# Pooled attention and an MLP on one core: k by halves of its heads on 96 partitions, v by DMAs of 128 partitions, the last row tile in parts

## Chip, core and metric

One core of a Trainium2 chip. The metric is the device time of one execution in microseconds (us); lower is better. All data lies in the chip's HBM at the start and the result has to be there at the end.

## What is computed

```python
B, H, S, D = 8, 8, 576, 64;  pool = 8                    # float32 inputs
k_p = k.reshape(B, H, S // pool, pool, D).mean(axis=3)   # 72 pooled rows per head
v_p = v.reshape(B, H, S // pool, pool, D).mean(axis=3)
scores = matmul(q, k_p.T) / sqrt(D)
attn = softmax(scores)
x = matmul(attn, v_p)            # 4608 tokens x 512, heads side by side
h = x @ w_in                     # 512 -> 2048
out = gelu_tanh(h) @ w_out       # 2048 -> 512, float32
```

## The kernel before, in words

The batch has 8 parts (b) of 576 tokens, 4608 tokens in all. The MLP works on 9 groups (g) of 512 tokens. For a group, p1 (`p1_mm`, L333) multiplies by w_in: 16 column tiles (fo) times 4 tiles of the contraction (ko), each a matmul of 128x512, with the Gelu on ACT after each fo. p2 (`p2_mm`, L344) multiplies by w_out: 4 row tiles (r) times 16 fo, and `store` (L348) copies a row tile out of PSUM on DVE and sends it to HBM by four DMAs of 32 rows. All of it is written out by hand: `tc.manual_schedule()` keeps each engine's instructions in the order in which the program issues them, so a wait holds whatever is behind it on that engine.

The attention of batch g + 1 is laid between the matmuls of group g: pooling of k and v on DVE and the transposes of k on TensorE during p1 (the dictionary `plan`, L463 and L466), scores, exponentials and products during p2 (the list `pos`, L501). Batch 0 has no group before it. It stands ahead of the loop (L364 to L434), and there TensorE is kept busy with matmuls that nobody reads (`spin`, L359).

Names that matter:

- `load_k`, `load_v`, `load_q` (L67 to L88) bring one batch's k, v, q. In k, 4 pooled rows' inputs (4 x 2 KB) lie on one partition of `kts` (128 partitions, columns 0 to 3); the remaining 64 rows and v's last pooled rows take a fifth column. v is loaded in two DMAs of 64 partitions each, the lower heads on partitions 0 to 63, the upper on 64 to 127. For batch 0 k and v are issued from SP and ACT and q from GpSimd (POOL), which converts to bfloat16 on the way; for all other batches everything is issued from POOL.
- POOL's queue after that (L107 to L113): w_in in two halves, k, q, v of batch 1, then w_out in four quarters. The first eight DMAs go out at once; a ninth waits until the first has landed, and so on, since eight semaphores are used in turn.
- `k_steps` (L141): three additions on DVE that fold 8 rows to 1, into `kps`. `trans_k_mm` (L170) transposes `kps` on TensorE, `trans_k_copy` (L176) copies the result into `kTs`, twice (e = 0 and 1), in six pieces each. `v_steps` (L155) folds v into `vps` (batch 0: `vz`); `v_moves` (L149), from SP, moves v's last pooled rows.
- Batch 0: `qk`/`expo` give the scores and exponentials of a head pair, `den0` the sums by a matmul with `ones`, `inverse0` 1/sum on ACT (logarithm and exponential), `av0` the product with v, `mult0` the multiply on DVE into `xT`. After the last `mult0` (L426) DVE clears buffers for the later batches (L427 to L434), and after those comes batch 1's `k_steps`.
- In group 0 the first two row tiles of p2 go by quarters of w_out (L516), so that each quarter is asked for as late as possible.

Of the kernel before, what the change touches and what calls it, by code (L numbers as in the profile page):

```python
# [8 lines left out]
F32 = mybir.dt.float32  # L9
# [9 lines left out]
def kernel(  # L19
# [9 lines left out]
    nc = tc.nc  # L29
# [13 lines left out]
    KR = 4  # L43
# [20 lines left out]

    kts = [consts.tile([128, KR + 1, 512], F32, name=f"kt{i}") for i in range(2)]

    def load_k(b, engs):  # L67
        rows = k[b].rearrange("h (j l) d -> (h j) (l d)", l=8)
        main = rows[0:128 * KR].rearrange("(p r) c -> p r c", r=KR)
        n = KR // len(engs)  # L70
        for i, eng in enumerate(engs):
            eng.dma_start(out=kts[b % 2][:, i * n:(i + 1) * n], in_=main[:, i * n:(i + 1) * n])
        engs[0].dma_start(out=kts[b % 2][64:128, KR], in_=rows[128 * KR:])
        rows = v[b].rearrange("h (j l) d -> j h (l d)", l=8)
        for i in range(2):
            engs[-1].dma_start(out=kts[b % 2][32 * i:32 * i + 32, KR], in_=rows[64:, 4 * i:4 * i + 4])

    def load_v(b, engs):
        rows = v[b].rearrange("h (j l) d -> j h (l d)", l=8)
        for i in range(2):  # L80
            engs[i % len(engs)].dma_start(out=vts[b % 2][64 * i:64 * i + 64], in_=rows[0:64, 4 * i:4 * i + 4])  # L81
# [16 lines left out]
    load_k(0, [nc.sync, nc.scalar])  # L98
    load_v(0, [nc.sync, nc.scalar])
    load_q(0, 0, 1)  # L100
    load_q(0, 1, 2)
# [7 lines left out]
    load_k(1, [nc.gpsimd])  # L109
    load_q(1)  # L110
    load_v(1, [nc.gpsimd])
    for i in range(4):
        nc.gpsimd.dma_start(out=w_out_b[:, 4 * i:4 * i + 4, :].rearrange("p j d -> p (j d)"), in_=w_out_v[:, i])  # L113
# [6 lines left out]
    kps = [consts.tile([128, KR + 2, D], BF16, name=f"kp{i}") for i in range(2)]  # L120
# [6 lines left out]
    nc.vector.memset(idle, 0.0)  # L127
    nc.vector.memset(kTs[0][0], 0.0)
# [9 lines left out]
    def add(o, a, b):  # L138
        nc.vector.tensor_tensor(out=o, in0=a, in1=b, op=ALU.add)  # L139

    def k_steps(b, c=slice(0, KR + 1)):  # L141


        t = kts[b % 2]
        return [lambda: add(t[:, c, 0:256], t[:, c, 0:256], t[:, c, 256:512]),
                lambda: add(t[:, c, 0:128], t[:, c, 0:128], t[:, c, 128:256]),
                lambda: add(kps[b % 2][:, c], t[:, c, 0:64], t[:, c, 64:128])]

    def v_moves(b):  # L149

        for i in range(2):
            nc.sync.dma_start(out=vps[b % 2][64 - 64 * i:72 - 64 * i, 4 * i:4 * i + 4, 0],
                              in_=kps[b % 2][32 * i:32 * i + 32, KR])
# [13 lines left out]
    def half_bank(bank):  # L167
        return PS[:, bank, :].bitcast(BF16)

    def trans_k_mm(b, bank, r0=0, r1=KR + 1, n=128):  # L170
        tp = half_bank(bank)[:, 0:(KR + 1) * 128].rearrange("p (r c) -> p r c", c=128)
        kf = kps[b % 2].rearrange("p r d -> p (r d)")
        for r in range(r0, r1):
            nc.tensor.transpose(out=tp[:n, r, :], in_=kf[:, r * D:r * D + n], identity=identb)  # L174

    def trans_k_copy(b, e, bank, lower=True, upper=True):  # L176


        tp = half_bank(bank)[0:D, 0:(KR + 1) * 128].rearrange("p (r c) -> p r c", c=128)
        o = kTs[b % 2][e][e * 64:(e + 1) * 64]  # L180
        copy = nc.vector.tensor_copy

        def heads(h0, h1, c0, j0, j1):
            copy(out=o[:, h0:h1, c0:c0 + (j1 - j0) * KR].rearrange("p h (j r) -> p h j r", r=KR),  # L184
                 in_=tp[:, 0:KR, h0 * KH:h1 * KH].rearrange("p r (h j) -> p h j r", j=KH)[:, :, j0:j1])

        if lower:
            heads(0, 4, 0, 0, KH)
        if upper:
            heads(4, H - 1, 64, 0, 16)  # L190
            heads(4, H - 1, 0, 16, KH)
            copy(out=o[:, H - 1, 64:72].rearrange("p (j r) -> p j r", r=KR),
                 in_=tp[:, 0:KR, (H - 1) * KH:128].rearrange("p r j -> p j r"))
            copy(out=o[:, H - 1, 72:128], in_=tp[:, KR, 64:120])
            copy(out=o[:, H - 1, 0:8], in_=tp[:, KR, 120:128])

    def trans_k(b, bank):
        trans_k_mm(b, bank)
        for e in range(2):
            trans_k_copy(b, e, bank)  # L200
# [143 lines left out]
    def p2_mm(g, r, fo):  # L344
        nc.tensor.matmul(out=PS[:, o_bank(g, r), :], lhsT=gTs[g][:, fo, r * 128:(r + 1) * 128], rhs=w_out_b[:, fo, :],  # L345
                         start=(fo == 0), stop=(fo == FO - 1))

    def store(g, r):  # L348
        osb = opool.tile([128, DM], F32, name="osb")
        nc.vector.tensor_copy(out=osb, in_=PS[:, o_bank(g, r), :])  # L350

        for n in range(4):
            b, c = divmod(g * GROUP + r * 128 + n * 32, S)
            rows = out[b * S:(b + 1) * S].rearrange("(p t e) d -> e t p d", t=TP, e=2)
            eng = nc.scalar if (g, r) == (NG - 1, 3) and n % 2 else nc.sync
            eng.dma_start(out=rows[c // CH, c % CH // 32], in_=osb[n * 32:(n + 1) * 32, :])
# [8 lines left out]
    spin(22, 1)  # L365
    for f in k_steps(0, slice(0, KR)):
        f()
# [5 lines left out]
    trans_k_mm(0, 4, 0, KR, D)  # L373
    trans_k_copy(0, 0, 4, upper=False)
    trans_q(0, *QG[0], 5, nc.scalar)
    trans_q(0, *QG[1], 6, nc.vector)
    trans_k_copy(0, 1, 4, upper=False)
# [3 lines left out]
    for f in k_steps(0, slice(KR, KR + 1)):  # L381
        f()
    scores(1, 0, 2)
    trans_k_mm(0, 4, KR, KR + 1, D)
    trans_k_copy(0, 0, 4, lower=False)

    for h in range(H):
        i = h // 4
        nc.tensor.matmul(out=PS[64 - 64 * i:72 - 64 * i, 7, h * D:(h + 1) * D],
                         lhsT=identb[0:64, 32 * i + h % 4:32 * i + 32:4], rhs=kps[0][0:64, KR],  # L390
                         start=True, stop=True)
# [9 lines left out]
    trans_k_copy(0, 1, 4, lower=False)  # L401
# [9 lines left out]
    spin(4, 4)  # L411
    av0(0, 0, 4)
    mult0(0, 0, 4)
    den0(0, 2, 2)
    inverse0(0, 2, 2)
    av0(1, 0, 0)
    mult0(1, 0, 0)
    spin(3, 6)
    den0(1, 2, 6)
    inverse0(1, 2, 6)  # L420
    spin(3, 4)
    av0(0, 2, 4)
    mult0(0, 2, 4)
    spin(3, 0)
    av0(1, 2, 0)
    mult0(1, 2, 0)  # L426
    for t in kps:  # L427
        nc.vector.memset(t[:, KR + 1], 0.0)
# [11 lines left out]
    for g in range(NG):  # L440
# [3 lines left out]
        def load_next():  # L444

            load_q(g + 2)
            trans_q_dma(g + 2)
            nc.gpsimd.tensor_copy(out=gate, in_=qTs[g + 2][0:1, 1, TP - 1, 0:2])  # L448
            load_k(g + 2, [nc.gpsimd])
            load_v(g + 2, [nc.gpsimd])  # L450
# [62 lines left out]
        seq = [(r, fo) for r in range(4) for fo in range(FO)]  # L513
# [3 lines left out]
        for m, (r, fo) in enumerate(seq):  # L517
            for f, a in todo.pop(m, []):
                f(*a)
            p2_mm(g, r, fo)  # L520
            if fo == FO - 1:
                store(g, r)
        for m in sorted(todo):
            for f, a in todo[m]:
                f(*a)

# [29 lines left out]
```

The softmax here doesn't subtract the row's maximum and nothing guards it: scores larger than these inputs give would overflow.

## Time and profile before

| | us |
|---|---|
| median of 3 runs | 308.79 (308.76 to 308.96) |
| the profiled execution | 308.29 |
| its span in the profile | 306.5 |
| TensorE busy | 298.2 (97% of the span) |
| ACT busy | 219.0 (71%) |
| DVE busy | 150.4 (49%) |
| POOL busy | 36.3 (12%) |
| first matmul of p1 starts | 22.08 |
| last matmul ends | 302.1 |

The 1.8 us between span and execution lie around what the profile shows. A busy TensorE is not a TensorE at its peak: the idle spins count as busy too. In the timeline a line has start, duration, engine, line of the kernel, operation, what is written and read, and in brackets the idle time ahead of it and what ended it. In the chain of waits a piece has start, duration and what the time went to. PE is TensorE, PEld its weight loads, DVE VectorE, ACT ScalarE, POOL GpSimd, SP SyncE; a q behind a name is the engine's own queue of DMAs and semaphores.

### The profile page before, as it was taken

The numbers are of one execution on the slowest core, as the hardware profiler recorded it, in microseconds if no ns is written. First come the engines' busy times: TensorE is split into PE (matmuls) and PEld (weight loads), VectorE is DVE, ScalarE is ACT, GpSimd is POOL, SyncE is SP. The second block draws the span as 40 slices with busy tenths as digits, with TensorE's granted clock in tenths as the row PEclk, the third lists the DMA queues.
The fourth block names the chain that finished last, engine by engine and source line by source line (L and its number), as shares of the span: only waits on it lengthen the run. The fifth ranks groups of instructions, "written<-read, shape, count | busy, mean of one in ns | idle before, by whom it ended". The sixth has DMA issues, their size and how long they took to land.

```text
span 306.5 us, 4325 instructions
## 1 busy us (share of the span) xinstructions
PE 298.2 (97%) x1518; PEld 157.4 (51%) x1548; DVE 150.4 (49%) x334; ACT 219.0 (71%) x402; POOL 36.3 (12%) x69
## 2 busy tenths in 40 slices
PE   8999999999999999999999999999999999999994
PEld 3555555555555555555555555555555555445441
DVE  5868557573677057806681559245933630110021
ACT  1686679868987798779977998789868987206400
POOL 7103002305004000220014000400000000000000
PEclk9999999999999999999999999999999999999999
DMA  7999996987957952596159725662101210121022
GB/s 225 266 257 253 214 186 137 299 176 177 269 146 167 247 122 51 114 282 156 34 112 266 168 56 106 200 151 71 35 1 36 63 41 2 34 70 34 2 70 68
DMA packets 30359, 41.12 MB, mean 134 GB/s; under 512 B 18113, under 2 KB 18113, under 8 KB 29441
## 3 DMA queue, kind: packets, MB, share of 16 engines
q0 software_dynamic: 7856, 25.43, 34.9%
q1 hardware_dynamic: 21888, 14.09, 19.2%
q10 hardware_dynamic: 592, 1.31, 1.2%
q8 instruction: 12, 0.20, 0.3%
q14 instruction: 11, 0.08, 0.1%
HBM read 36.70 MB, written 9.44 MB: 151 GB/s over the span
## 4 chain that ended last, share of the span: by engine, by line
PE 83%; DMA 12%; POOL 1%; issue 1%; ACT 0%; DVE 0%; POOLq 0%
PE PS L345 38%; PE PS L336 36%; DMA kt<-in_k_dram 7%; DMA w_out_b<-in_moe_w_out_dram 5%; PE PS L239 4%; PE PS L261 4%; PE PS L174 1%; POOL w_in_b L105 0%; POOL qb L86 0%; POOL w_out_b L113 0%; DVE osb L350 0%; ACT e L247 0%; ACT ld L269 0%; ACT ld L268 0%; POOL identb masks.py:199 0%
## 5 line engine op out<-in xcount | busy, mean ns | idle before, releaser
L345 PE MATMUL PS<-w_out_b,gT 128*128 128x512 bf16 x560 | 134.2, 379 | 0.9
L336 PE MATMUL PS<-xT,w_in_b 128*128 128x512 bf16 x563 | 126.2, 379 | 0.6
L342 ACT ACTIVATE gT<-PS 128x512 bf16<-128x512 f32 x144 | 81.1, 604 | 47.5 <-PE PS L336 47.4
L336 PEld LDWEIGHTS <-w_in_b 128*128 128x128 bf16 x576 | 64.7, 113 | 57.2
L345 PEld LDWEIGHTS <-gT 128*128 128x128 bf16 x576 | 56.1, 97 | 56.7 <-issue 1.1
L350 DVE COPY osb<-PS 128x512 f32<-128x512 f32 x36 | 24.9, 691 | 98.3 <-PE PS L345 95.3
L279 DVE TENSOR_TENSOR xT<-PS,rc 64x288 bf16<-64x288 f32 x112 | 51.0, 455 | 31.6 <-ACT rc L271 29.3
L247 ACT ACTIVATE e<-PS 72x576 bf16<-72x576 f32 (+1 forms) x64 | 41.0, 646 | 9.1 <-PE PS L239 8.2
L239 PE MATMUL PS<-qT,kT 128*72 128x288 bf16 (+1 forms) x128 | 25.9, 286 | 0.9 <-ACT qT L214 0.6
L271 ACT ACTIVATE rc<-ld 128x288 f32<-128x288 f32 x56 | 24.8, 443 | 1.8
L314 ACT ACT_TABLE_LOAD x17 | 21.8, 1283 | 4.3 <-issue 4.1
L268 ACT ACTIVATE ld<-PS 64x288 f32<-64x288 f32 x56 | 22.8, 407 | 1.3
L269 ACT ACTIVATE ld<-PS 64x288 f32<-64x288 f32 x56 | 22.5, 402 | 1.3
L261 PE MATMUL PS<-e,vp 72*128 72x288 bf16 (+1 forms) x112 | 23.1, 286 | 0.0
L139 DVE TENSOR_TENSOR kt<-kt 128x1280 f32<-128x1280 f32 (+5 forms) x18 | 18.8, 1044 | 5.5 <-DMA kt<-in_v_dram 2.6
L239 PEld LDWEIGHTS <-kT 128*72 128x72 bf16 (+1 forms) x128 | 13.2, 105 | 15.2 <-DVE qT L216 1.2
L448 POOL COPY gate<-qT 1x2 bf16<-1x2 bf16 x6 | 1.0, 174 | 140.0 <-DMA qT<-qb 140.0
L139 DVE TENSOR_TENSOR vt<-vt 128x1024 f32<-128x1024 f32 (+1 forms) x16 | 15.3, 956 | 1.8 <-DMA vt<-in_v_dram 1.5
L184 DVE COPY kT<-PS 64x288 bf16<-64x288 bf16 (+2 forms) x48 | 13.0, 319 | 6.2 <-PE PS L174 6.1
L362 PE MATMUL PS<-idle 128*128 128x512 bf16 x39 | 11.9, 447 | 1.2 <-DVE idle L127 1.2
L261 PEld LDWEIGHTS <-vp 72*128 72x128 bf16 (+1 forms) x112 | 11.0, 98 | 3.8
L81 POOL DMA_DIRECT2D vt<-in_v_dram x14 | 9.0, 655 | 7.5 <-DMA w_in_b<-in_moe_w_in_dram 5.5
(47 smaller groups left out, 90.0 us busy)
## 6 DMA issues: line engine op xcount, KB each, us to landing
out_dram<-osb SPq DMA_DIRECT2D x142, 64.0 KB
kt<-in_k_dram POOLq DMA_DIRECT2D x7, 1024.0 KB, 6.2
vt<-in_v_dram POOLq DMA_DIRECT2D x14, 512.0 KB, 8.6
qb<-in_q_dram POOLq DMA_DIRECT2D x7, 576.0 KB, 11.6
w_in_b<-in_moe_w_in_dram POOLq DMA_DIRECT2D x2, 1024.0 KB, 16.7
w_out_b<-in_moe_w_out_dram POOLq DMA_DIRECT2D x4, 512.0 KB, 13.9
kt<-in_k_dram POOLq DMA_DIRECT2D x7, 128.0 KB, 5.9
kt<-in_v_dram POOLq DMA_DIRECT2D x14, 64.0 KB, 5.7
```

The lines of the kernel that those rows point to most:

```text
L139: nc.vector.tensor_tensor(out=o, in0=a, in1=b, op=ALU.add)
L239: nc.tensor.matmul(out=PS[:n, bank + e, :CH].rearrange("j (t p) -> j t p", p=32), lhsT=kTs[b % 2][c][:, h, :n], rhs=qTs[b][:, h // 4, :, h ...
L247: nc.scalar.activation(out=e[:n], in_=PS[:n, bank:bank + 2, :CH], func=ACT.Exp, scale=1.0 / 64.0)
L261: nc.tensor.matmul(out=PS[:, bank + x, :CH], lhsT=window(vps[b % 2][:n], 2 * pr + x), rhs=e[:n, x, :], start=True, stop=True)
L268: nc.scalar.activation(out=ld[0:64], in_=PS[64:128, bank, :CH], func=ACT.Ln)
L269: nc.scalar.activation(out=ld[64:128], in_=PS[0:64, bank + 1, :CH], func=ACT.Ln)
L271: nc.scalar.activation(out=rc, in_=ld, func=ACT.Exp, scale=-1.0)
L279: nc.vector.tensor_tensor(out=xT[rows, pr, col:col + CH], in0=PS[rows, bank + x, :CH], in1=rc[rows], op=ALU.mult)
L336: nc.tensor.matmul(out=PS[:, h_bank(g, fo), c0:c1], lhsT=w_in_b[fo // 8][:, ko, q * 512 + j:(q + 1) * 512:4], rhs=xT[:, ko, r0 + c0:r0 + c ...
L342: nc.scalar.activation(out=gTs[g][:, fo, :], in_=PS[:, h_bank(g, fo), :], func=ACT.Gelu_apprx_tanh)
L345: nc.tensor.matmul(out=PS[:, o_bank(g, r), :], lhsT=gTs[g][:, fo, r * 128:(r + 1) * 128], rhs=w_out_b[:, fo, :], start=(fo == 0), stop=(fo ...
L350: nc.vector.tensor_copy(out=osb, in_=PS[:, o_bank(g, r), :])
```

## The change

- **k.** Three pooled rows' inputs lie on a partition now, so each half of the heads takes 96 partitions. The lower heads go to partitions 0 to 95, columns 0 to 2; the upper heads to partitions 32 to 127, columns 3 to 5. v's last pooled rows are on partitions 0 to 31, columns 3 and 4. For batch 0 the lower half is issued from SP and ACT, beside q's first half from POOL; the upper half follows q's first half on POOL. The parts of `kts` that no load writes are cleared by DVE.
- **Pooling and transposes of k.** The additions take 3 columns per half in batch 0, and 6 columns otherwise (5 before). There are 6 transposes per batch instead of 5; the copies are 5 pieces instead of 6.
- **Batch 0's order.** q's first half is transposed before k, both copies of it on ACT; 13 + 3 spins instead of 22 at the start; k's upper half is summed where the fifth column was; one `den0`/`inverse0` pair moves ahead of the first `av0`, and the spins between the later products become fewer.
- **v.** Four DMAs, one for a head of each half, of 128 partitions.
- **w_out.** Its first quarter is issued ahead of batch 1's v.
- **The last row tile** of the last group: columns 0 to 383 for all fo, then 384 to 511, each with its own copy and stores. The first part's four stores go to SP, the second part's to SP and ACT by turns.

```diff
-    KR = 4
+    KR = 3
     KH = Sp // KR
...
+    kts = [consts.tile([128, 2 * KR, 512], F32, name=f"kt{i}") for i in range(2)]
+    K0 = (0, 32)
+
+    def load_k(b, i, engs):
+        rows = k[b].rearrange("(i h) (j r l) d -> i (h j) (r l d)", i=2, r=KR, l=8)[i]
+        n = 4 * KH // len(engs)
+        for x, eng in enumerate(engs):
+            eng.dma_start(out=kts[b % 2][K0[i] + x * n:K0[i] + (x + 1) * n, KR * i:KR * i + KR],
+                          in_=rows[x * n:(x + 1) * n].rearrange("p (r c) -> p r c", r=KR))
+
+    def load_v_last(b, eng):
         rows = v[b].rearrange("h (j l) d -> j h (l d)", l=8)
         for i in range(2):
-            engs[-1].dma_start(out=kts[b % 2][32 * i:32 * i + 32, KR], in_=rows[64:, 4 * i:4 * i + 4])
+            eng.dma_start(out=kts[b % 2][0:32, KR + i], in_=rows[64:, 4 * i:4 * i + 4])
 
     def load_v(b, engs):
-        rows = v[b].rearrange("h (j l) d -> j h (l d)", l=8)
-        for i in range(2):
-            engs[i % len(engs)].dma_start(out=vts[b % 2][64 * i:64 * i + 64], in_=rows[0:64, 4 * i:4 * i + 4])
+        rows = v[b].rearrange("(i h) (j l) d -> h i j (l d)", i=2, l=8)
+        for h in range(4):
+            engs[h % len(engs)].dma_start(out=vts[b % 2][:, h], in_=rows[h, :, 0:64])
...
-    load_k(0, [nc.sync, nc.scalar])
+    load_k(0, 0, [nc.sync, nc.scalar])
+    load_q(0, 0, 1)
+    load_k(0, 1, [nc.gpsimd])
+    load_v_last(0, nc.scalar)
+    load_q(0, 1, 2)
     load_v(0, [nc.sync, nc.scalar])
-    load_q(0, 0, 1)
-    load_q(0, 1, 2)
...
-    load_k(1, [nc.gpsimd])
+    load_k_all(1)
     load_q(1)
-    load_v(1, [nc.gpsimd])
     for i in range(4):
+        if i == 1:
+            load_v(1, [nc.gpsimd])
         nc.gpsimd.dma_start(out=w_out_b[:, 4 * i:4 * i + 4, :].rearrange("p j d -> p (j d)"), in_=w_out_v[:, i])
...
+    nc.vector.memset(kts[0][0:32, 2 * KR - 1], 0.0)
...
     act_set(EXP_SET)
-    spin(22, 1)
-    for f in k_steps(0, slice(0, KR)):
+    spin(13, 1)
+    for f in k_steps(0, 0, 1):
         f()
...
-    trans_k_mm(0, 4, 0, KR, D)
-    trans_k_copy(0, 0, 4, upper=False)
     trans_q(0, *QG[0], 5, nc.scalar)
-    trans_q(0, *QG[1], 6, nc.vector)
-    trans_k_copy(0, 1, 4, upper=False)
+    trans_q(0, *QG[1], 6, nc.scalar)
+    spin(3, 4)
+    trans_k_mm(0, 0, 4)
+    trans_k_copy(0, 0, 0, 4)
+    trans_k_copy(0, 1, 0, 4)
     scores(0, 0, 2)
     scores(0, 1, 0)
     spin(2, 7)
-    for f in k_steps(0, slice(KR, KR + 1)):
+    for f in k_steps(0, 1, 2):
         f()
     scores(1, 0, 2)
-    trans_k_mm(0, 4, KR, KR + 1, D)
-    trans_k_copy(0, 0, 4, lower=False)
+    trans_k_mm(0, 1, 4)
+    trans_k_copy(0, 0, 1, 4)
...
     inverse0(1, 0, 6)
-    spin(4, 4)
+    spin(2, 4)
+    den0(0, 2, 2)
+    inverse0(0, 2, 2)
+    spin(2, 4)
     av0(0, 0, 4)
     mult0(0, 0, 4)
-    den0(0, 2, 2)
-    inverse0(0, 2, 2)
+    den0(1, 2, 6)
+    inverse0(1, 2, 6)
     av0(1, 0, 0)
     mult0(1, 0, 0)
-    spin(3, 6)
-    den0(1, 2, 6)
-    inverse0(1, 2, 6)
-    spin(3, 4)
     av0(0, 2, 4)
     mult0(0, 2, 4)
-    spin(3, 0)
+    spin(2, 0)
     av0(1, 2, 0)
     mult0(1, 2, 0)
     for t in kps:
-        nc.vector.memset(t[:, KR + 1], 0.0)
+        nc.vector.memset(t[:, 2 * KR], 0.0)
+    for t in kts:
+        nc.vector.memset(t[96:128, 0:KR], 0.0)
+    nc.vector.memset(kts[1][0:32, 2 * KR - 1], 0.0)
...
-            eng = nc.scalar if (g, r) == (NG - 1, 3) and n % 2 else nc.sync
-            eng.dma_start(out=rows[c // CH, c % CH // 32], in_=osb[n * 32:(n + 1) * 32, :])
+            eng = nc.scalar if c1 == DM and c0 and n % 2 else nc.sync
+            eng.dma_start(out=rows[col // CH, col % CH // 32, :, c0:c1], in_=osb[n * 32:(n + 1) * 32, c0:c1])
...
+        seq = [(r, fo) for r in range(4 if g + 1 < NG else 3) for fo in range(FO)]
...
+    for c0, c1, bank in ((0, 384, o_bank(g, 3)), (384, DM, 4)):
+        for fo in range(FO):
+            p2_mm(g, 3, fo, bank, c0, c1)
+        store(g, 3, bank, c0, c1)
```

## The prediction

> **What bounds the kernel now.** I read the page's chain first, then the chain of waits between 20 and 46 us, then the timeline of the first 41 us, then the end.
>
> ```profile
> PE 83%; DMA 12%; POOL 1%; issue 1%; ACT 0%; DVE 0%; POOLq 0%
> ```
>
> ```profile
> 4.55 21.57 DMA kt<-in_k_dram
> 27.46 16.53 DMA w_out_b<-in_moe_w_out_dram
> 43.99 0.04 issue
> 44.03 0.81 PE PS L345 x3
> ```
>
> From 44 us to the last matmul TensorE decides; its time there is a fixed amount of matmuls, so a gain must come before 44 us or after the last matmul (302.1 us). At 44.03 TensorE starts on the last quarter of w_out 0.04 us after it landed: the DMA stream holds the first group. Nothing before 44 us pays unless that stream is earlier too. The windows (columns as in the page's header line; the last two are DMA share and GB/s written) show where the stream is slow:
>
> ```profile
> 22.00:24.00 2.00, 1.95 (x10) 1.09 (x10) 1.54 (x5) 0.73 (x1) 0.56 (x1) 1.00 1.01 421
> 28.00:30.00 2.00, 2.00 (x11) 1.04 (x10) 1.97 (x3) 1.32 (x3) 0.72 (x2) 1.00 1.02 194
> 30.00:32.00 2.00, 2.00 (x11) 1.02 (x9) 1.17 (x2) 1.42 (x3) 0.00 (x0) 1.00 1.03 223
> ```
>
> The engines are full in all three. At 22 to 24 us k of batch 1 arrives (4-byte data, 128 partitions) at 421 GB/s. At 28 to 32 us v of batch 1 arrives, also without a cast, in DMAs of 64 partitions: 194 and 223 GB/s. (w_out's own 207 to 220 GB/s is no fault: it reads 4 bytes for 2 written.)
>
> The start of the main work, and VectorE's queue behind it:
>
> ```profile
> 8.61 0.68 PE L204 MATMUL PS<-identb,qb 128*128 128x128 bf16 x9
> 10.29 2.56 ACT L247 ACTIVATE e<-PS 72x576 bf16<-72x576 f32 x4 [0.49 <-PE PS L239]
> 20.94 0.81 PE L362 MATMUL PS<-idle 128*128 128x512 bf16 x3
> 22.08 8.15 PE L336 MATMUL PS<-xT,w_in_b 128*128 128x512 bf16 x36
> 22.35 0.76 DVE L308 TENSOR_TENSOR xT<-PS,rc 128x576 bf16<-128x576 f32 x1 [0.38 <-PE PS L304]
> 24.43 0.91 DVE L432 MEMSET vp<- 128x1024 bf16 x1 [0.16 <-issue]
> 28.40 2.28 DVE L139 TENSOR_TENSOR kt<-kt 128x1280 f32<-128x1280 f32 x2
> 34.67 0.44 PE L174 MATMUL PS<-identb,kp 128*128 128x128 bf16 x5
> 40.11 0.87 DVE L139 TENSOR_TENSOR vp<-vt 64x256 bf16<-64x256 f32 x2
> 40.69 0.41 PE L261 MATMUL PS<-e,vp 72*128 72x288 bf16 x2
> ```
>
> Between 17 and 22 us TensorE is full, but partly with idle spins (L362). VectorE goes without a pause from the last multiply (22.35) through the memsets to batch 1's k sums (28.40 to 31.20). At 40.11 it writes batch 1's pooled v, whose first half TensorE uses at 40.69: VectorE is the second limit, with no slack there.
>
> **What the Trainium skill says.** "SBUF — State Buffer", section "Door 1: The DMA port swizzle": partitions 0 to 63 reach only 8 of 16 DMA ports, 196 GB/s against 328 for 128 partitions at 1 MiB. The 194 to 223 against 421 GB/s above agree in kind. "DMA: Bandwidth & Descriptors", section "Queues, rings and completion order": each DMA engine takes turns between the queues that have work, so a transfer of GpSimd's queue shares with SP's and ACT's. The trace's packet records show the first q packet only at 4.75 us, as the k packets end, and turns from there. "VectorE: DVE Perf Modes", section "Zero memsets can be issued as uint32 (trn2)": a memset costs a cycle per element whatever the type. The trace agrees: 0.48 us for 512 elements, 0.91 for 1024. "TensorE: Matmul & The Clock Gate", section "Wait — 56ns, not 53.3ns?": 128 columns start every 56 ns. Here five transposes take 0.28 us of the chain.
>
> **The change part by part.**
>
> Start. Ahead of q on the DMA engines now stand 0.59 MB of k instead of 1.05 MB (at the 289 to 329 GB/s of 2 to 6 us, 1.4 us less). If q's first half follows k as it did, it moves from 8.6 us to 7.2 (bound: unchanged, 8.6); with its queue ready by about 3 us and fewer k packets in the turns it may reach 6.3. I take 6.8. k's lower sums scale from 128x1024 1.23, 128x512 0.69 and 128x256 0.42 to 0.96, 0.56, 0.36: done near 6.5, ahead of q. Then transposes 0.5, two copies on ACT 0.69 and 0.58 (the second leaves VectorE), meanwhile three spins, k transposes, the kT copy 0.45: first exponential near 9.4 (10.29 before). The upper half of k follows q in GpSimd's queue, 0.59 MB at about 0.24 MB/us (its share when q came): 9.2. Its sums now cost 1.8 us for 768 elements (before 0.98 for 256), and the queue of TensorE waits behind them: the fourth exponential comes at about 12.0, some 0.2 earlier than before. So the early start is nearly used up; after that VectorE (0.65 copy, 0.85 cast, 0.82 q copies, 0.65 copy, v sums to the first half 2.35) gives pooled v at 16.65 instead of 17.15.
>
> Order of the last products. Behind that TensorE had four av groups, two den groups and nine spins until 22.08 (4.9 us). Now one den group stands earlier and only two spins remain; 3.8 us with the waits for the multiplies (0.76 each): p1 starts at 20.45. ACT no longer waits 0.34 and 0.27 us for the den groups, its last reciprocal ends near 20.55, and the last multiply, call its end M, is at 21.35 instead of 23.11.
>
> VectorE after M. Added: two memsets of 1536 elements (0.48 and 0.91 extrapolate to 1.35, 1.48 from start to start) and one of 512 (0.55): 3.5 us. k sums of six columns instead of five: 3.27 against 2.80. So k is ready at M + 5.3 + 3.5 + 3.3 = M + 12.1 = 33.45; TensorE would be there 12.6 after its start, at 33.05, and waits 0.4. This is queued ahead of p1's last eight matmuls, and Gelu with it. From there the VectorE chain to pooled v is 6.15 us: av at M + 18.25 = 39.6, against 40.69: 1.09 us gained of the 1.76 at M.
>
> DMA stream. v of batch 1 at the full rate saves 1.05 MB/0.21 - 1.05 MB/0.40 = 2.4 us, so w_out's last quarter lands at 41.6 instead of 43.99, and TensorE asks for it at about 42.5: no wait. Before, TensorE waited about 0.22 us for each of two quarters: 0.44 gained. The 96-partition k (3 rows of 2 KB each) costs about the same port time as before. More GpSimd issues (four v instead of two, 0.65 each) lie under a stream that is always full; SP gets no new issue in the middle.
>
> Later batches. One more k transpose in each of six: 6 x 0.056 = 0.34 lost on TensorE. Their added 0.5 us of k sums is hidden: at 92.8 us the sums are done 3.5 us before the transposes (96.26).
>
> End. The last row tile: 16 matmuls of 384 columns and 16 of 128, 16 x (0.162 + 0.056), as before within 0.05. The final copy is 128 columns, 0.29 instead of 0.69. But SP has four issues for the first part, about 0.45 each, from 0.3 before to 1.5 us after the last matmul, and then two more; its last issue begins 1.95 after it instead of 1.1. Landing follows issue as before. Cost 0.8, less the smaller packets and the closing checks that may no longer follow: between 0 and 0.6, I take 0.35.
>
> Sum: -1.09 - 0.44 + 0.34 + 0.35 = -0.84. In short: M - 22.2. The profiled execution took 308.29 (span 306.5 and 1.8 around it), the median is 308.79, 0.5 more; 308.79 - 0.84 = 307.95, say 307.9. 0.2% is 0.6 us, about what a measurement of this kernel can tell from no change.
>
> **The rivals.** (1) Slower: q is not earlier. If GpSimd's first transfer begins at 4.75 us for a reason of its own, q is there at 8.4 and k's upper half at 10.3. The 1.8 us of sums then come 1.1 later than reckoned, M is about 23.0, and VectorE's extra memsets are paid in full: 23.0 - 22.2 = +0.8, 309.6. For it: the first GpSimd transfer needs 3.5 us to its first packet, others 1.3. Against: its first packets come just as k's end. It is slower from M above 22.8. (2) The weights still hold the first group: v is no faster, the last quarter lands at 43.99 and everything before is lost: 0.34 + 0.35, 309.5; with half the saving about 308.8. For: all DMA slices are full. Against: 421 beside 194 GB/s. (3) More is gained: q at 6.3 makes M 20.9, and the end costs nothing: -1.6, 307.2.
>
> **How the numbers follow.** Forecast 0.50 (its own range 307.2 to 308.6), rival 1 0.22, rival 2 0.18, rival 3 0.10. Faster: 0.37 of the forecast and rival 3, 0.47. Same: 0.13 of the forecast, 0.08 of rival 2, 0.04 of rival 1, 0.25. Slower: 0.28. The range for 8 in 10 runs from 306.9 (below rival 3) to 309.7 (rival 1).
>
> **What would show it.** In the profile after: q's transposes near 6.8 and not 8.6; the upper k sums near 9.2; the last multiply ending near 21.4; p1 starting near 20.5; memsets of 32x1536 of about 1.35 us; a wait of TensorE for VectorE at batch 1's k transposes (33.0 to 33.5); about 400 GB/s while v of batch 1 arrives; w_out's end no longer in the chain; the last SP issue about 2 us after the last matmul. I am wrong if M is above 22.2, if the chain still holds w_out at 44 us, or if some later stage waits that does not now.

## The result, and the profile after

| | before | after |
|---|---|---|
| median of the runs (lowest to highest) | 308.77 us (308.32 to 308.96) | 350.11 us (349.16 to 351.20) |
| ratio, 95% interval | | 1.134 [1.130, 1.138] |
| span of the profiled execution, mean granted clock | 306.5 us, 0.999 | 348.8 us, 0.936 |
| first matmul of w_in (p1) | 22.08 us | 63.34 us |
| last matmul ends | 302.1 us | 344.5 us |

The forecast was 307.9 us, the range ended at 309.7. The change costs 41.3 us. In the profile 41.3 us lie ahead of p1 and 1.1 us behind it, so the place to look is the first batch. First the page: busy tenths of TensorE and its granted clock in 40 slices of 8.7 us, and the chain by engines.

```profile
PE   4840002989999999999999999999999999999995
PEclk9685555999999999999999999999999999999999
PE 74%; DMA 9%; another core or an unknown queue 6%; DVE 4%; ACT 3%; issue 1%; ACTq 1%; DVEq 0%
```

TensorE is idle in slices 4 to 6, and its clock has fallen to half. The same two lines of the kernel before (slices of 7.7 us):

```profile
PE   8999999999999999999999999999999999999994
PEclk9999999999999999999999999999999999999999
```

The chain of waits (start, length, what) says on what TensorE waits:

```profile
3.51 31.26 DMA vt<-in_v_dram
34.82 21.04 another core or an unknown queue
73.65 1.77 DVE kt L153
```

The first two pieces are 52 us together, and both are waits for v of batch 0: the second, for which the profile names no source, ends at 55.86, just before VectorE starts on `vt` at 55.98. No piece of w_out is left in the chain, but only because everything else is later. The timeline, with the lines that answer to those of before:

```profile
8.83 0.68 PE L223 MATMUL PS<-identb,qb 128*128 128x128 bf16 x9 [3.30 <-DMA qb<-in_q_dram]
11.67 1.19 ACT L266 ACTIVATE e<-PS 72x576 bf16<-72x576 f32 x2 [1.17 <-PE PS L258]
11.97 1.55 DVE L153 TENSOR_TENSOR kt<-kt 128x768 f32<-128x768 f32 x2 [0.60 <-DMA kt<-in_v_dram]
55.98 1.95 DVE L153 TENSOR_TENSOR vt<-vt 128x1024 f32<-128x1024 f32 x2 [37.42 <-DMA vt<-in_v_dram]
58.45 1.14 PE L323 MATMUL PS<-e,vz 72*128 72x288 bf16 x4 [36.96 <-DVE vz L153]
63.34 4.91 PE L355 MATMUL PS<-xT,w_in_b 128*128 128x512 bf16 x21
63.61 0.76 DVE L327 TENSOR_TENSOR xT<-PS,rc 128x576 bf16<-128x576 f32 x1 [0.45 <-PE PS L323]
64.81 1.34 DVE L453 MEMSET kt<- 32x1536 f32 x1 [0.36 <-issue]
73.65 2.75 DVE L153 TENSOR_TENSOR kt<-kt 128x1536 f32<-128x1536 f32 x2
77.05 0.51 PE L192 MATMUL PS<-identb,kp 128*128 128x128 bf16 x6 [0.95 <-DVE kp L153]
```

In the kernel before VectorE came to v here:

```profile
14.72 1.95 DVE L139 TENSOR_TENSOR vt<-vt 128x1024 f32<-128x1024 f32 x2
```

In the timeline of after, read the idle time in brackets: VectorE waits 37.42 us for v, TensorE 36.96 us for the pooled v that comes of it. q's transposes start at 8.83 us (before 8.61, forecast 6.8), the upper k sums at 11.97 (forecast 9.2). From p1 on the distances are nearly those forecast (M, the end of the last multiply, is 64.37; the transposes of batch 1's k start at M + 12.7, forecast M + 12.1).

The windows (start and end, length, then busy us and count of PE, PEld, DVE, ACT and POOL, then granted clock, DMA share and GB/s) show DMA engines that are no longer full, and at times nearly empty:

```profile
30.00:32.00 2.00, 0.00 (x0) 0.00 (x0) 0.00 (x0) 0.00 (x0) 0.00 (x0) 0.50 0.64 123
34.00:36.00 2.00, 0.00 (x0) 0.00 (x0) 0.00 (x0) 0.00 (x0) 0.00 (x0) 0.50 0.13 37
38.00:40.00 2.00, 0.00 (x0) 0.00 (x0) 0.00 (x0) 0.00 (x0) 0.28 (x2) 0.50 0.29 67
```

A share of 0.13 is two engines of sixteen. The trace's packet records fit: from 12 to 49 us SP's and ACT's queues each move only some 6 packets of 2048 bytes per us, at 84 to 96 ns (medians) a packet.

**The theory.** The Trainium skill, "DMA: Bandwidth & Descriptors", section "Why a DMA increments its semaphore by 16 and not by 1", says how many engines carry a DMA: the largest number up to 16 that divides the slowest dimension (not 1) of both access patterns; on SP's and ACT's queues they are the lowest-numbered ones, and each posts one increment of the semaphore at its end. The new v DMA reads `rows[h]` as (i, j, (l d)): its slowest dimension is i = 2. By the rule two engines carry it, and all four DMAs use the same two. Call this A. Rivals: B, 2 KB rows from two distant places are slow on any number of engines; C, the two hardware queues starve behind GpSimd's queue, which got q and half of k earlier; D, the half clock or the order of k's halves holds the start, and v is a bystander.

### The profile page after: what moved, and what is told of

The parts are those of the page before. It is cut to its first block, busy times and chain, and to the rows that moved or that the text cites. A ratio compares the mean times of both kernels' runs of the same rounds, so it can differ in the third digit from the quotient of the medians.

```text
span 348.8 us, 4365 instructions
## 1 busy us (share of the span) xinstructions
PE 299.1 (86%) x1530; PEld 159.5 (46%) x1559; DVE 156.9 (45%) x322; ACT 219.5 (63%) x403; POOL 50.4 (14%) x84
## 3 DMA queue, kind: packets, MB, share of 16 engines
q0 software_dynamic: 20960, 26.12, 36.1%
## 4 chain that ended last, share of the span: by engine, by line
PE 74%; DMA 9%; another core or an unknown queue 6%; DVE 4%; ACT 3%; issue 1%; ACTq 1%; DVEq 0%
PE PS L364 33%; PE PS L355 31%; DMA vt<-in_v_dram 9%; PE PS L258 4%; PE PS L280 4%; DVE kt L153 1%; PE PS L192 1%; DVE kt L453 1%; PE PS L323 1%; ACT ld L288 1%; ACT ld L287 1%; ACT e L266 1%; ACTq L79 1%; ACT gT L361 1%
## 5 line engine op out<-in xcount | busy, mean ns | idle before, releaser
L364 PE MATMUL PS<-w_out_b,gT 128*128 128x512 bf16 (+2 forms) x578 | 134.0, 373 | 0.7
L364 PEld LDWEIGHTS <-gT 128*128 128x128 bf16 x592 | 57.1, 98 | 55.6 <-issue 0.4
L373 DVE COPY osb<-PS 128x512 f32<-128x512 f32 (+2 forms) x37 | 25.1, 677 | 100.9 <-PE PS L364 97.8
L323 PE MATMUL PS<-e,vz 72*128 72x288 bf16 (+1 forms) x16 | 3.8, 392 | 37.0 <-DVE vz L153 37.0
L258 PE MATMUL PS<-qT,kT 128*72 128x288 bf16 (+1 forms) x128 | 26.9, 296 | 0.8 <-DVE kT L203 0.5
L315 ACT ACTIVATE rc<-ld 128x576 f32<-128x576 f32 x4 | 2.7, 682 | 38.4 <-DVE xT L327 38.3
L85 POOL DMA_DIRECT2D vt<-in_v_dram x28 | 22.6, 839 | 25.5 <-DMA w_in_b<-in_moe_w_in_dram 21.7
L153 DVE TENSOR_TENSOR kt<-kt 128x768 f32<-128x768 f32 (+4 forms) x18 | 22.0, 1224 | 2.6 <-DMA kt<-in_k_dram 1.5
L203 DVE COPY kT<-PS 64x252 bf16<-64x252 bf16 (+4 forms) x80 | 16.3, 266 | 7.7 <-PE PS L192 7.6
```

The costliest lines, as they stand in the source:

```text
L258: nc.tensor.matmul(out=PS[:n, bank + e, :CH].rearrange("j (t p) -> j t p", p=32), lhsT=kTs[b % 2][c][:, h, :n], rhs=qTs[b][:, h // 4, :, h ...
L364: nc.tensor.matmul(out=PS[:, bank, c0:c1], lhsT=gTs[g][:, fo, r * 128:(r + 1) * 128], rhs=w_out_b[:, fo, c0:c1], start=(fo == 0), stop=(fo ...
L373: nc.vector.tensor_copy(out=osb[:, c0:c1], in_=PS[:, bank, c0:c1])
```

## The experiments

Ratios are to the kernel before on the same chip, with 95% intervals. The runs are spread over five chips, so compare ratios rather than medians. p1 and the last matmul are from each run's one profile (before: 22.08 and 302.1). In e4, e12 and e16 batch 0's rows stand elsewhere than the computation reads them; only their times are used.

| run | edit | median us | ratio | p1 at | last matmul ends |
|---|---|---|---|---|---|
| e1_v_old | after, v as before | 314.09 | 1.0157 [1.0125, 1.0188] | 28.16 | 309.4 |
| e2_v_new | before, new v | 345.76 | 1.1185 [1.1157, 1.1212] | 59.92 | 339.5 |
| e3_v0_old | after, batch 0's v as before | 319.33 | 1.0306 [1.0273, 1.0338] | 27.00 | 314.1 |
| e4_v0_eight | after, batch 0's v by 8 heads | 320.78 | 1.0398 [1.0353, 1.0442] | 28.47 | 318.1 |
| e5_warm | e1, 23 spins for 13 | 315.39 | 1.0196 [1.0168, 1.0224] | 26.09 | 309.1 |
| e6_v_gpsimd | e1, batch 0's v on GpSimd | 318.25 | 1.0290 [1.0247, 1.0334] | 27.51 | 311.0 |
| e7_v_last_behind | e1, last rows of v behind v | 316.99 | 1.0250 [1.0221, 1.0279] | 29.78 | 310.9 |
| e8_memsets_gpsimd | e6, memsets on GpSimd | 317.92 | 1.0289 [1.0250, 1.0328] | 27.51 | 312.7 |
| e9_tail_only | before, last tile in parts | 309.03 | 1.0009 [0.9996, 1.0023] | 22.32 | 302.9 |
| e10_order_tail | e9, order of the last products | 308.91 | 1.0010 [0.9999, 1.0022] | 20.89 | 303.3 |
| e11_k_pitch | e5, k's rows 528 apart | 314.08 | 1.0178 [1.0157, 1.0198] | 24.88 | 307.4 |
| e12_k_aligned | e5, batch 0's k on 128 partitions | 314.13 | 1.0169 [1.0138, 1.0201] | 27.22 | 308.5 |
| e13_k_upper_hw | e5, k's upper half on SP, ACT | 313.01 | 1.0114 [1.0092, 1.0136] | 25.81 | 306.9 |
| e14_k_upper_hw_ms | e13, memsets on GpSimd | 312.20 | 1.0098 [1.0077, 1.0119] | 24.59 | 306.4 |
| e15_q_both_first | e6, k's upper half behind q | 317.29 | 1.0262 [1.0231, 1.0293] | 28.21 | 311.1 |
| e16_aligned_hw | e13, batch 0's k on 128 partitions | 310.43 | 1.0056 [1.0032, 1.0080] | 22.97 | 304.1 |
| e17_late_w_in | e5, memsets on GpSimd before w_in | 314.38 | 1.0178 [1.0154, 1.0201] | 26.17 | 307.3 |
| e18_order_stream | e10, batch 1's v behind w_out's first quarter | 308.92 | 0.9994 [0.9977, 1.0012] | 20.95 | 304.3 |

### v's form: e1 to e4

e1_v_old, the change with v taken back:

```diff
-        rows = v[b].rearrange("(i h) (j l) d -> h i j (l d)", i=2, l=8)
-        for h in range(4):
-            engs[h % len(engs)].dma_start(out=vts[b % 2][:, h], in_=rows[h, :, 0:64])
+        rows = v[b].rearrange("h (j l) d -> j h (l d)", l=8)
+        for i in range(2):
+            engs[i % len(engs)].dma_start(out=vts[b % 2][64 * i:64 * i + 64], in_=rows[0:64, 4 * i:4 * i + 4])
```

> The changed kernel with one part undone: v is loaded as before, in two DMAs of 64 partitions (rows of one position, then four heads), for all batches; k by halves, the new order, the memsets and the divided last row tile stay. Theory A (the new v DMA has only two entries in its outermost dimension of HBM and is therefore carried by two of the sixteen DMA engines): v of batch 0 lands near 15 to 18 us again, no fall of the granted clock after 18 us, time 307.5 to 310; that is my forecast without the v gain, 308.3 to 308.8, if its other steps hold. Theory C (the two hardware queues starve behind GpSimd's queue because q and k's upper half were moved ahead, whatever v's form): v still lands after 40 us, 335 to 350. Theory D (the cold clock or the order of k does it): first products still late, above 320.

e2_v_new puts the three removed lines into the kernel before, in place of the three added ones.

> The kernel before with one part of the change alone: v in four DMAs of 128 partitions (outermost two head halves). Theory A: v of batch 0 lands near 50 us or later, and the time is 345 to 355. Theory B (the row pattern of 2 KB pieces from two distant places is slow by itself, on all engines): also 340 to 355, so this run does not part A from B. Theories C and D: v lands below 25 us, time 307 to 312.

e1: 314.09 us; some 36 of the 41 us are gone, so C and D fall as the main cause. e2: 345.76 us, v's sums start at 50.83 us: v's form alone is enough. But e1 is 5 us above its forecast; what that is made of comes below.

e3_v0_old takes the old form for batch 0 alone, e4_v0_eight another form for batch 0:

```diff
+        if b == 0:
+            rows = v[b].rearrange("h (j l) d -> h j (l d)", l=8)
+            for x in range(4):
+                engs[x % len(engs)].dma_start(out=vts[b % 2][:, x], in_=rows[:, 16 * x:16 * x + 16])
+            return
```

> The changed kernel, batch 0's v alone loaded as before (two DMAs of 64 partitions on SP and ACT), the later batches' v in the new form on GpSimd's queue. Theory A: batch 0 is not late, no cold clock; in the later batches the new form on two engines each is late only if a group of 31.8 us does not cover it, so the time is within 1 us of the run with v undone everywhere, or above it by what batch 1's v holds up w_out's quarters behind it (0 to 3 us): 308 to 312. My prediction's step (v of batch 1 at twice the rate) would make it about 0.4 us faster than the run with v undone everywhere. Theories C and D: above 320.

> The changed kernel, batch 0's v in four DMAs of 128 partitions on the same two queues, with the same 2 KB rows and the same bytes, but cut so that the outermost dimension of HBM is the eight heads (sixteen positions of each) instead of two head halves; the rows of batch 0's v land in other places than the computation wants, so batch 0's output is not the reference's; nothing else is changed. Theory A: eight engines carry each DMA, v of batch 0 is there by 16 to 20 us, time within 3 us of the run with only batch 0's v undone: 308 to 315. Theory B (rows of 2 KB from distant places, or 128 partitions, are slow by themselves): v lands after 35 us, 330 to 350. Theories C and D: 335 to 350.

The trace holds a record of each increment of a DMA's semaphore, and so of the time at which each engine ended its share of the DMA (an engine end). For batch 0's v on SP and ACT:

| kernel | slowest dimension | engine ends per DMA | v's sums start |
|---|---|---|---|
| e3 (2 DMAs) | 64 | 16 | 20.13 us |
| e4 (4 DMAs) | 8 | 8 | 22.52 us |
| after (4 DMAs) | 2 | 2 | 55.98 us |

The last ends of the four in the profile after lie at 28.6, 34.8, 50.2 and 55.9 us; in e3 the last of the two is at 17.4. All of this passes through the same two engines: from 34 to 36 us SP's, ACT's and GpSimd's queues move 12 or 13 packets each, and the share is 0.13. GpSimd's transfers are held up by it too: of the sixteen ends of w_in's halves fourteen are there by 17.4 and 23.4 us, the last two only at 27.0 and 37.1. An estimate from the packets: v's 512 at 84 to 96 ns would keep two engines busy for 22 to 25 us; the rest of the 52 us I put down to turns with GpSimd's packets.

Packets of the same 2 KB from as distant places, in DMAs to the same 128 partitions, are no trouble on eight engines: B falls, A stands. The skill's rule agrees here with the number of ends: 16, 8 and 2.

Both times, e3's and e4's, were forecast too low by the 5 us of e1 and by the later batches: measured side by side, e3 is 5.2 us above e1 (4.6 by the ratios), though only the later batches' v, on GpSimd's queue, is in the new form. The windows of e3 while v of batch 1 arrives, and then its timeline:

```profile
36.00:38.00 2.00, 2.00 (x11) 1.02 (x9) 1.73 (x4) 1.47 (x3) 0.16 (x1) 1.00 0.94 214
38.00:40.00 2.00, 1.70 (x14) 1.02 (x13) 1.97 (x2) 1.19 (x3) 0.72 (x1) 1.00 1.01 230
40.00:42.00 2.00, 1.29 (x12) 0.87 (x13) 1.97 (x7) 0.16 (x1) 0.00 (x0) 1.00 1.09 226
```

```profile
46.42 1.95 DVE L158 TENSOR_TENSOR vt<-vt 128x1024 f32<-128x1024 f32 x2 [2.25 <-DMA vt<-in_v_dram]
48.31 2.72 PE L369 MATMUL PS<-w_out_b,gT 128*128 128x512 bf16 x6 [2.90 <-DMA w_out_b<-in_moe_w_out_dram]
```

214 to 230 GB/s, not the 400 that I had reckoned, and about the 194 to 223 of the old form in the kernel before. The last engine of batch 1's v ends at 46.3 us (44.2 in e1), and w_out's next quarter, behind v in the queue, comes 2.9 us late. TensorE's clock falls to 0.5 in the pause, so that the six products behind it take 2.72 us where six take 1.46 in e1. A wait of 1.35 us for batch 2's pooled v at 85 us, which e1 does not have, makes up most of the rest.

### The other parts alone: e9, e10, e18

e9_tail_only and e10_order_tail are the kernel before with these parts of the change and nothing of k and v. e18_order_stream moves one line more:

```diff
-    load_v(1, [nc.gpsimd])
     for i in range(4):
+        if i == 1:
+            load_v(1, [nc.gpsimd])
```

> The kernel before with one part of the change alone: the last row tile's second product in parts of 384 and 128 columns, stored apart. My prediction put 0.35 us on it, bounds 0 and 0.6 (ratio 1.001, at most 1.002). If the shorter last copy gains more than SP's four added issues cost, the ratio is below 1; if those issues stand in the way fully, 0.8 us, 1.0026.

> The kernel before with the last row tile in parts and the changed order of batch 0's last products (the third denominator ahead of the first product, 4 idle spins in place of 13); k and v as before. The prediction: TensorE needs about 1.1 us less between pooled v and p1, so p1 starts near 21.0 instead of 22.1 and VectorE's chain is 1.1 us earlier; but w_out's last quarter still lands near 44 us, so hardly anything of it is seen at the end: ratio 0.998 to 1.002. If w_out does not hold the first group, 1.1 - 0.35 = 0.75 us are gained: 0.9975. If the end costs more than thought, up to 1.003.

> The kernel of e10_order_tail (k and v as before, new order of the last products, last tile in parts) with batch 1's v behind the first quarter of w_out in GpSimd's queue, as the change has it. In e10_order_tail TensorE waited 1.69 us for w_out's first quarter and 0.32 for two others. The first quarter now comes some 5 us earlier, v by as much as a quarter takes later. If the stream's end holds the first group, nothing is gained in sum: ratio 0.999 to 1.002. If the first quarter alone held it, 0.995 to 0.998.

e9 costs 0.3 us (the interval takes in zero), as priced. e10 is the clean test of two steps of the prediction. About 1.1 us was worked out, and p1 starts 1.19 us earlier than before and 1.43 earlier than in e9. (Before and e9 have the same work up to p1; that they differ by 0.24 us is the noise of one profile.) Nothing of it is seen at the end. Its list of waits (engine, line, releaser: us in total, times, longest) says why:

```profile
PE PS L345 <- DMA w_out_b<-in_moe_w_out_dram: 2.3, 3, 1.7
```

The weights hold the first group: rival 2 of the prediction. In e18 TensorE does not wait for the first quarter, but for the three others, 3.5 us in all: same time. e18 is the best version that these runs point to, and it is level with the kernel before.

### What stays: k and the start, e5 to e8 and e11 to e17

In e1 TensorE has no work from 6.2 to 10.4 us, because 9 spins were taken out for a q that did not come earlier. Its timeline has q's transposes and k's upper sums here:

```profile
10.41 1.14 PE L223 MATMUL PS<-identb,qb 128*128 128x128 bf16 x9 [4.20 <-DMA qb<-in_q_dram]
14.40 1.55 DVE L153 TENSOR_TENSOR kt<-kt 128x768 f32<-128x768 f32 x2 [0.22 <-DMA kt<-in_k_dram]
```

In the windows of e1 the granted clock is 0.89 at 8 to 9 us and 0.50 from 9 to 22 us.

e5_warm has `spin(23, 1)` in place of `spin(13, 1)`. e6_v_gpsimd moves `load_v(0, ...)` behind make_identity on GpSimd's queue. e7_v_last_behind moves `load_v_last(0, nc.scalar)` behind `load_v(0, ...)`. e8_memsets_gpsimd takes e6 and puts the three memsets of `kts` on GpSimd, behind its issues of w_in.

> The changed kernel with v as before (the kernel of the run e1_v_old), and 23 idle spins instead of 13 at the start, so that TensorE is busy until q's first half lands (about 10.4 us). In e1_v_old TensorE was idle from 6.2 to 10.4 us and its granted clock fell to 0.5 until 22.9 us; from q's arrival to the first matmul of w_in took 17.75 us there, 13.47 us in the kernel before. If the cold clock is what makes that stretch long, p1 starts 3.5 to 4 us earlier (24.2 to 24.7 instead of 28.16) and the time is 310 to 311; if other waits fill the stretch, p1 stays above 27 and the time above 313.

> The kernel of e1_v_old, with batch 0's v (two DMAs of 64 partitions) issued on GpSimd's queue behind q's second half instead of on SP and ACT: nothing but k's lower half and the last rows of v shares the DMA engines with q's first half. If v on the hardware queues is what delays q (taking turns with it, and writing the same ports), q's first transposes start at 6.3 to 7.2 us as the prediction had it, the clock stays up, p1 starts at 20 to 21.5, time 307 to 309.5. If q is late for another reason (the start of GpSimd's first transfer, k's upper half behind it on the same queue), q stays above 8.5 us and the time at 310 to 314.

> The kernel of e1_v_old with the last rows of v moved behind v in ACT's queue, so that v's two halves (partitions 0 to 63 from SP, 64 to 127 from ACT) start together and not the lower one alone. If the load on partitions 0 to 63 alone held q's last packets, q's transposes start at 8 to 9 us and the time is 310 to 312. If it is the turns between three busy queues, q stays at 10 to 11 us; the last rows of v then come later, k's upper sums with them, and the time is 314 to 316.

> The kernel of e6_v_gpsimd, with the three added memsets of k's tiles (3.2 us on VectorE after the last multiply) on GpSimd instead, behind its issues of w_in. My prediction reckoned 3.5 us of VectorE's chain and a wait of TensorE of 0.4 us for it (0.94 in e1_v_old): 0.4 to 1.1 us faster than e6_v_gpsimd. If the end of w_out's stream holds the first group instead, no difference (within 0.3 us).

Misses, most of them. e5 brings p1 from 28.16 to 26.09, less than forecast, and the time does not follow. What comes late next in its profile: TensorE waits 0.6 us for w_out's quarters (none in e1), and in the second group this:

```profile
67.51 2.75 DVE L153 TENSOR_TENSOR kt<-kt 128x1536 f32<-128x1536 f32 x2 [3.74 <-DMA kt<-in_v_dram]
70.91 0.51 PE L192 MATMUL PS<-identb,kp 128*128 128x128 bf16 x6 [0.74 <-DVE kp L153]
```

Batch 2's k sums wait for the last rows of v, two small DMAs at the end of the stream. So the transfers hold p1's gain here as they do in e10. e6 shows that v on SP and ACT is not what keeps q from the forecast's 6.8: without it q is there at 8.50 us, 1.9 us earlier than in e1, but no better than before; v and the last rows of v then come too late. e7: q at 10.38, so it is not the load on partitions 0 to 63 either. e8: TensorE's wait for k of batch 1 (0.94 us in e6) is gone, its wait for w_out grows from 1.69 to 3.36 us instead, the time is the same.

The trace's increments for q's first half: in the kernel before its sixteen engine ends lie between 7.39 and 8.30 us. In e6 thirteen lie between 5.84 and 6.80 us, where the prediction had q, and the last three at 7.72, 8.16 and 8.46. A transfer is there when its last engine is. Three tries at that, and at k's late upper half (`...` stands for lines left out):

```diff
 e11_k_pitch
-    kts = [consts.tile([128, 2 * KR, 512], F32, name=f"kt{i}") for i in range(2)]
+    kts = [consts.tile([128, 2 * KR, 528], F32, name=f"kt{i}") for i in range(2)]
...
 e12_k_aligned (batch 0; load_v_last goes to a tile of its own)
+            flat = k[b].rearrange("(i h) s d -> i (h s d)", i=2)[i].rearrange("(p c) -> p c", p=128)
+            to = kts[0].rearrange("p r c -> p (r c)")[:, 1536 * i:1536 * i + 1152]
...
 e13_k_upper_hw
     load_k(0, 0, [nc.sync, nc.scalar])
+    load_k(0, 1, [nc.sync, nc.scalar])
     load_q(0, 0, 1)
-    load_k(0, 1, [nc.gpsimd])
```

> The kernel of e5_warm with one size changed: the rows of k's tile are 528 elements apart instead of 512, so that a partition's three rows are no longer one run of 6144 bytes but three of 2048, on the same 96 partitions by the same DMAs. In the runs so far with k in 96 partitions, packets of 6144 bytes took 290 to 430 ns where 235 were expected, q's half landed on its last engine 2.4 to 4.7 us after its first (before: 0.9), and every transfer beside them was slower. Theory L (the long packets make the other queues wait): with 2048-byte packets q is there by 8 to 8.5 us, k's upper half by 11, p1 starts 1.5 to 2.5 us earlier than in e5_warm (26.1), ratio 1.010 to 1.014. Theory P (96 partitions do not stand in step with the sixteen engines' own partitions, so engines write each other's ports): nothing gained, ratio 1.018 to 1.025.

> The kernel of e5_warm, with batch 0's k in the same two halves of the same bytes, but written to all 128 partitions (4608 bytes each; the lower half in two DMAs of 2304) instead of 96; batch 0's k values and last rows of v then stand in other places than the computation reads, so batch 0's output is not the reference's; the rest is unchanged. Theory P: the sixteen engines end within 1 to 1.5 us of each other again, q's first transposes start at 7.2 to 8.5 us, k's upper half is there by 10.5, p1 starts at 22 to 24, ratio 1.005 to 1.013. Theory L: the lower half has short packets, the upper half long ones: q earlier by about 1 us only, ratio 1.014 to 1.018. If neither k's form nor its packets matter (q is late because v and k's upper half come early), as e5_warm: 1.018 to 1.022.

> The kernel of e5_warm with k's upper half issued on SP and ACT right behind the lower half, not on GpSimd's queue behind q's first half. If the lateness of k's upper half (13.2 us in e5_warm, its sums hold the transposes, the upper scores and everything queued behind them) is what costs the 5 us, it now lands by 6.5 to 7.5, q at 8.3 to 9 as in the kernel before, p1 starts at 20.9 to 22.3, and the ratio is 1.000 to 1.006 (what is left: a wait of 0.94 at batch 1's k transposes and 0.34 us of added transposes). If the 96-partition form of k or the order of the work costs it wherever it stands, p1 stays above 24 and the ratio above 1.012.

e11 lies between the theories: q's transposes at 8.44, p1 at 24.88, but k's lower sums only at 7.46 (5.12 in e5); its interval overlaps e5's. e12: the lower k sums start at 4.35 instead of 5.12, q at 8.95; its interval overlaps e5's too. Both miss the gain forecast, and neither settles anything alone, because k's upper half behind q is still late in both (sums at 12.07 and 13.09).

e13 takes that away: 1.0114 [1.0092, 1.0136] against e5's 1.0196 [1.0168, 1.0224]. Four tenths of e5's excess, then, hang on the upper half's place on GpSimd's queue, but hardly by way of the start. The upper half has its last end at 8.45 us; its sums still start only at 13.04 (13.25 in e5), since q now comes later (10.39) and holds what is ahead of them, and p1 comes just 0.3 us earlier. Of the 2.2 us gained at the last matmul 1.9 lie behind p1, where e5's waits for w_out (0.6 us) and for batch 2's k (0.74) are gone. A further part is tested by e16_aligned_hw, which is e13 with e12's form of k:

> The kernel of e13_k_upper_hw with batch 0's k, the same bytes by the same two queues, written to 128 partitions instead of 96 (as in e12_k_aligned; batch 0's k values and last rows of v stand in other places than the computation reads, so batch 0's output is not the reference's). If the 96-partition form is what loads slowly, k's halves are there by 4.4 and 6.5 us (5.5 and 8.5 in e13), q by 8.3 to 9 (10.4), p1 starts 1.5 to 2.5 us earlier than in e13 (25.8), ratio 1.003 to 1.008. If not, as e13: 1.010 to 1.013.

The windows of e13, and then of e16, while k of batch 0 arrives on the same two queues, the same bytes:

```profile
2.00:5.00 3.00, 3.00 (x9) 1.06 (x8) 1.67 (x7) 0.36 (x1) 2.93 (x6) 1.00 0.98 248
```

```profile
2.00:5.00 3.00, 3.00 (x8) 1.06 (x7) 2.52 (x8) 0.33 (x1) 2.92 (x6) 1.00 0.99 367
```

The engines are busy all the time in both (0.98 and 0.99), yet they move 248 GB/s in e13 and 367 in e16. In e13 each half's 96 partitions are filled by two DMAs of 48, in e16 all 128 by each DMA. The last end of k is at 8.45 us in e13 and 5.91 in e16, q is there at 10.39 and 8.94, p1 starts at 25.81 and 22.97; 1.8 us of time by the ratios. That settles that k's form costs it.

The packets show it directly: a KB of k on SP and ACT takes 67 ns in e13 and 45 in e16 (50 in e12), 61 to 65 in after, e1 and e5, and 46 in the kernel before. e16 changes the length of the runs with the number of partitions (6144 to 2304 bytes), but in e11 the runs are 2048 bytes, and a KB still takes 60 to 62 ns, with k's lower half later, not earlier: the partitions, not the runs. Nor is it the cut into 48: k of the batches after the first two, in one DMA of 96 partitions a half on GpSimd's queue, takes 61 to 62 ns a KB in e1, e13 and e16, against 49 in the kernel before. Why is argued only: the skill ("DMA: Bandwidth & Descriptors", section "The descriptor swizzle") says that in a transfer to 128 partitions each engine writes a port of its own; engines that get three or six partitions each would not keep to that. No run shows the ports.

e14_k_upper_hw_ms is e13 with the memsets on GpSimd; e15_q_both_first is e6 with k's upper half behind q's second; e17_late_w_in is e5 with the memsets on GpSimd ahead of its issues of w_in:

> The kernel of e13_k_upper_hw with the three added memsets of k's tiles on GpSimd instead of VectorE. If VectorE's chain holds the first group there, 0.7 to 1.1 us faster than e13_k_upper_hw (ratio 0.997 to 1.003); if w_out's last quarter holds it (as in e10_order_tail, where TensorE waited 2.3 us for w_out), no difference within 0.3 us.

> The kernel of e6_v_gpsimd with k's upper half behind q's second half in GpSimd's queue instead of between q's halves. If the packets of k's upper half hold q's last three engines, q's first half lands by 6.8 to 7.3 us on its last engine (8.46 in e6_v_gpsimd); if something else does, at 8 to 9 us again. k's upper half comes later either way, the time is 1 to 3 us above e6_v_gpsimd.

> The kernel of e5_warm with the three added memsets on GpSimd instead of VectorE, ahead of its issues of w_in, so that these start near 6.5 us and not at 3.5. If GpSimd's issuing of w_in holds q's last engines (some of q's packets took 0.8 to 1.5 us instead of 0.19 between 4.2 and 5.4 us), q's first half ends at 7 to 7.5 us on all sixteen, p1 starts by 24, ratio 1.010 to 1.014. If not, q is late again (9 to 10 us), and the memsets alone are gained: 1.015 to 1.018.

e14 takes TensorE's wait for k away and gets a wait for w_out of 1.03 us (none in e13); 0.8 us of gain, within both intervals: not settled in time, but the wait that takes over is again the stream's. e15: fifteen of q's ends by 7.17, the last at 8.31, without k's upper half beside it; and the time is not above e6's, as had been expected. e17: the last at 8.84 although GpSimd issues nothing for w_in before 6.86 us. So neither is the cause of q's last engines. Between 4.2 and 5.4 us some of q's packets take 0.8 to 1.5 us instead of 0.19 in the profile after and in e1, e6 and e12; in before, e13 and e16 there are none, but in e11 there are none either, and q's last ends lag all the same. What holds them stays open.

## Why the prediction was wrong, point by point

- **v's form, the step that failed.** "v of batch 1 at the full rate" and, unsaid, batch 0's v in time. I took the count of partitions for the measure of a DMA's speed: 421 GB/s with 128, 194 with 64. The port section of the skill that I cited tells one of two conditions; I did not ask how many engines carry the DMA. Instead of -0.44 us: for batch 0 about 32 us by the ratios (after against e3), for the later batches about 5 (e3 against e1). Not 0.40 but at most 0.23 MB/us arrived, about as in the old form, and the last engine ended 2.1 us later than with it.
- **The bound of that step.** Rival 2 had "v is no faster" as its worst case. The new form was not in the trace of before, and I bounded it from one side only; no rival had v slower. So the slowest case was rival 1, 309.6, and the range ended at 309.7.
- **"Ahead of q stand 0.59 MB instead of 1.05".** Right in bytes, wrong in time: "the 96-partition k costs about the same port time" failed: 60 to 67 ns a KB against 46 in before, and 248 GB/s (e13) against 367 (e16). In after and e1 k's lower sums start 0.4 to 0.7 us before those of the kernel before (5.40 and 5.07 against 5.80), where 1.4 less was counted ahead of q. Half of q's engines did end by 6.3 us (e6); the last did not. Forecast 6.8; 8.83 after, 8.2 to 10.6 in the experiments with the new k. Rival 1 came true in this, through another mechanism: q's first packet does go earlier (4.1 us after and in e6, before 4.75).
- **k's upper half at 9.2 us.** Its sums start at 11.97 after and at 13.25 in e5. All the transposes and scores behind them in TensorE's queue follow.
- **Fewer spins.** Priced at nothing, covered by a q at 6.8. Without that cover the clock is at 0.5 from 9 to 22 us in e1; restoring the spins moves p1 by 2.1 us, but the time is not lower (e5).
- **The order of the last products: right.** 1.1 us forecast, 1.19 to 1.43 in e10. "Their gain of 1.09 at av": wrong in its place, since w_out held the first group (2.3 us of waits). This was rival 2, at 0.18.
- **VectorE after M: right in size.** Memsets 1.34 instead of 1.35 us. In e1 M is 29.2 and TensorE starts on k at 41.85, M + 12.7 (forecast 12.1); TensorE waits 0.94 instead of 0.4.
- **The tail and the later batches: right in size.** 0.28 for 0.35 (e9, interval -0.1 to 0.7); six transposes take 0.51 us where five took 0.44.

From the kernel after back to the one before, the runs make a chain: 32 us from after to e3 (batch 0's v), 4.6 to e1 (the later batches' v), 1.3 to e13 (k's upper half and the spins), 1.8 to e16 (k on 48 or 96 partitions), 1.7 to before, all by the ratios, times 308.8 us. They add up to 41.4 by construction, so the sum proves nothing; each step is as sure as its two intervals. Those of e1 and e13 overlap, so the 1.3 alone is not settled (from e5, which differs from e13 in the upper half's place only, it is 2.5). Of what e16 keeps, p1 is 0.9 us late; behind it lie the wait of 0.94 us for k of batch 1, the added transposes and the tail.

## What to carry to other kernels

Before a DMA is reshaped, write down its slowest dimension on both sides: it sets how many engines carry it; here two engines took until 56 us for the megabyte that sixteen had brought by 17, beside the same other transfers. Count partitions only after that, and do not take 96 for 128: here a KB of k took 60 to 67 ns instead of 45 to 50. Where a stream of transfers is full up to the point where the work waits for it, an earlier start of the work may buy nothing, as in e10; look which transfer is waited for next before pricing the gain.

## What the runs showed that was not expected

- The new form of v on GpSimd's queue brings 12,544 more packets of 8 bytes (448 for each of 28 DMAs), 9 ns each (median). The page's line for GpSimd's queue has 20960 packets in after and 8192 in e1, for 26.12 and 26.02 MB.
- A DMA's landing is its slowest engine. In e6 thirteen of sixteen ends were there at 6.8 us, the last at 8.46, and q's transposes started at 8.50.
- After a pause TensorE's clock came back at very different speeds. In the kernel after it was back at 62 us, 3.6 us after the first product at 58.45, with TensorE busy without a gap from 59 us on. In e1 it stayed at 0.50 from 9 to 22 us; there TensorE worked again from 10.4 us, but with gaps of 0.2 to 0.5 us (10.7 us busy of the 12 from 10 to 22). That the gaps are the reason is argued, not tested.
